# A linear-attention and two-layer expert kernel: decayed state on ScalarE from the ninth block on, a new step list, and another order at the end

## The chip, the cores and the metric

The kernel runs on one core of one Trainium2 chip. The metric is the device time of one execution in microseconds (us). Of the kernel before there are three timed runs, 505.46, 508.73 and 507.02 us, median 507.02. One further execution, of 505.58 us, was profiled; every row below is from it.

## The reference

Three things follow on each other. First, for 4 sequences and 8 heads of 768 tokens and 48 channels, a recurrent attention with a decay per channel:

```
cur   = (u * k_t) outer v_t
y_t   = r_t @ (state + cur)
state = w_t[:, None] * state + k_t outer v_t
```

Its output, 3072 tokens of 384 channels, goes through `h = x @ w_in` (384 to 2048), `g = h * cos(h)` and `x = g @ w_out`. Last comes a soft mixture of 8 experts with 4 slots each: `logits = x @ phi`; a softmax over all tokens gives each slot a mean of the tokens, each expert does `max(slot @ w1, 0) @ w2` (384 to 1024 to 384), and a softmax over the slots, token by token, mixes the 32 slot outputs into the output, 3072 x 384.

All inputs are float32 but `w_in`, `w_out` (float64, read as pairs of int32 and converted on the chip).

## The kernel before, in words

**Tiles and stages.** The 3072 tokens are 24 blocks of 128; a sequence has six blocks, a block two chunks (c) of 64 tokens. Two blocks make one of 12 groups of the softmax. Work on a block has three parts.

- *Attention of block j*: loads of r, k, v, w (`lr`, `lk`, `lv`, `lz`, `lw`, on SP's queue), transposes (`wT`, `rT`, `kT`, `kN` on PE), two scans of the decay on DVE (`scan`, `sp`), scaled keys and queries (`ks`, `L`), the chunk's inner products (`A`, then `mask`), the chunk's contribution to the state (`U` on PE). The state is carried by three small steps: `z` (line 250 on, the multiplication in L257) multiplies the state by the chunk's decay, `st` (L265, DVE) adds `U` to it, `rz` (L262, two ACT copies) puts z beside v for the product `y` (L276, PE). At the start of a sequence z is a memset (L254).
- *First layer of block t*: four quarters q of 512 columns. `h` (L430 to 432, nine PE matmuls), `turns` (L445, ACT), `rest` (L449, DVE), `cos` (L453, ACT), `mul` (L457, DVE), transposes `gT` (L464, PE), their copy `gc` (L470, ACT; some of the last on DVE), and `l` (L479, PE), the logits through a product of `w_out` and `phi`. `h` has two PSUM banks until nearly the end.
- *Softmax of group g*: `sum`, `lc`, `max`, `exp`, `dT`, `dc`, `ltok`; `E` (L575, PE) adds the tokens up with their weights, and `es` (L581, DVE) keeps the running sum `e_sb` and (L583) its divisor `st_s`. For the last group E and its update come in two halves (`E.11.0`, `E.11.1`, `esl.11.0`, `esl.11.1`).

**The order.** No planner runs: HEAD is a list of some 1900 steps written out in the file. Each step issues its instructions at its place, and each of the five engines (PE, DVE, ACT, POOL, and SP, which issues the DMAs) works through its own in that order. So an instruction waits for its data and for every earlier one on its engine. The name of a step holds its block, and then the chunk, quarter or part. The first steps also decode the weights: `raw` (load), `q` and `abs` (ACT), `d2a` (L343) and `d2b` (L348) on DVE, `whi`, `wn`, `wc` for `w_in`; `oT`, `oc`, `om` and others for `w_out`.

**The end.** After HEAD comes a second ordered part. PE adds up the divisor (`sum`, L729), transposes `e_sb` (L732), multiplies by `w_out` (L742) and transposes the slots' inputs (L749). `hidden(e)` (L761) does the first layer of expert e in 24 matmuls; `hidden_t(i)` takes the relu of four experts (L768, ACT), transposes it (L770, PE) and copies it (L772). `weights` (L719 to 721) rounds the token weights of one of four sets and one of two halves into `cr`, with a copy on ACT, DVE and POOL each. `expert_out(i, e)` (L801) is the second layer of expert e in 16 matmuls, for the columns 0 to 255 (i = 0) or 256 to 383 (i = 1). `slots_out` and `slots_round` (L808, L813, L814) sum it up and split it into a rounded part and a rest. `outputs(i, n0)` (L832, L834) mixes the slots for two tiles of 128 tokens (i = 0) or four (i = 1), copies the bank to `ob` (L841) and issues a store (L842). The expert weights are loaded whole, 1536 KB each (`load_e`, L642 and L646): numbers 0 to 5 when attention's memory is free (`att`), 6 to 10 into the memory of `w_in` and of x (`we`), 11 to 13 after HEAD, 14 and 15 during `hidden`.

## Time and profile before

| | |
|---|---|
| runs, us | 505.46, 508.73, 507.02; median 507.02 |
| profiled execution, us | 505.58 |
| its span, first to last instruction, us | 503.9 |
| busy: PE, DVE, ACT, POOL, us | 470.7, 420.2, 329.6, 101.9 |
| mean granted TensorE clock | 0.993 |
| largest groups: `h`, three lines, us | 118.2, 112.4, 112.7 |
| moved by DMA, MB | 67.47 |

Busy time is the time in which an engine ran at least one instruction. A matmul's end is modelled, so a busy PE is not one at its peak. Idle time counts only on the engine that is the bound in its stretch; so the tables by stretch say more than the shares over the whole span. A line's "idle before" is the time for which its engine stood still ahead of it, and the name behind the arrow is what ended that.

### The profile page before, as it was taken

The numbers are of one execution on the slowest core, as the hardware profiler recorded it, in microseconds if no ns is written. First come the engines' busy times: TensorE is split into PE (matmuls) and PEld (weight loads), VectorE is DVE, ScalarE is ACT, GpSimd is POOL, SyncE is SP. The second block draws the span as 40 slices with busy tenths as digits, with TensorE's granted clock in tenths as the row PEclk, the third lists the DMA queues.
The fourth block names the chain that finished last, engine by engine and source line by source line (L and its number), as shares of the span: only waits on it lengthen the run. The fifth ranks groups of instructions, "written<-read, shape, count | busy, mean of one in ns | idle before, by whom it ended". The sixth has DMA issues, their size and how long they took to land.

```text
span 503.9 us, 15604 instructions
## 1 busy us (share of the span) xinstructions
PE 470.7 (93%) x6521; PEld 369.3 (73%) x6521; DVE 420.2 (83%) x820; ACT 329.6 (65%) x724; POOL 101.9 (20%) x127
## 2 busy tenths in 40 slices
...
GB/s 220 307 259 240 142 206 163 101 50 81 35 92 27 103 2 124 67 43 62 57 89 56 23 75 48 50 95 64 49 22 27 407 277 57 110 404 305 398 138 276
DMA packets 145157, 67.47 MB, mean 134 GB/s; under 512 B 127168, under 2 KB 133568, under 8 KB 145088
## 3 DMA queue, kind: packets, MB, share of 16 engines
...
q14 instruction: 18, 0.15, 0.1%
...
## 4 chain that ended last, share of the span: by engine, by line
PE 66%; DVE 21%; ACT 6%; DMA 3%; issue 2%; SPq 0%; DVEq 0%; ACTq 0%
PE h L430 10%; PE h L432 9%; PE h L431 9%; PE gT L464 7%; PE l L479 4%; PE y L276 4%; PE E L575 3%; DVE lt L223 3%; DVE g L449 3%; DVE g L457 2%; PE A L197 2%; PE hps L761 2%; PE so L801 2%; DVE pt L159 2%; PE U L248 2%
## 5 line engine op out<-in xcount | busy, mean ns | idle before, releaser
L430 PE MATMUL h<-wu,x 128*128 128x512 f32 (+1 forms) x288 | 118.2, 411 | 1.0 <-DVE g L457 0.7
L432 PE MATMUL h<-wu,x 128*128 128x512 f32 (+1 forms) x288 | 112.7, 391 | 0.0
L431 PE MATMUL h<-wu,x 128*128 128x512 f32 (+1 forms) x288 | 112.4, 390 | 0.0
L453 ACT ACTIVATE g<-g,half_pi 128x512 f32<-128x512 f32 x97 | 69.4, 719 | 37.0 <-DVE g L449 36.3
L445 ACT ACTIVATE g<-h 128x512 int32<-128x512 f32 x96 | 56.9, 595 | 45.1 <-PE h L432 40.6
L457 DVE TENSOR_TENSOR g<-g,h 128x512 f32<-128x512 f32 x96 | 64.9, 679 | 13.2 <-ACT g L453 12.1
L449 DVE SCALAR_TENSOR_TENSOR g<-g,h 128x512 f32<-128x512 int32 (+1 forms) x96 | 64.6, 677 | 9.6 <-ACT g L445 8.6
L430 PEld LDWEIGHTS h<-wu,x 128*128 128x128 f32 x288 | 54.2, 188 | 15.0 <-DVE g L457 4.0
L211 POOL TENSOR_SCALAR_AFFINE_SELECT lt<-bo 64x512 f32<-64x512 f32 x48 | 36.6, 763 | 140.9 <-ACT bo L239 71.5
L432 PEld LDWEIGHTS h<-wu,x 128*128 128x128 f32 x288 | 54.1, 188 | 11.9
L431 PEld LDWEIGHTS h<-wu,x 128*128 128x128 f32 x288 | 54.3, 188 | 9.3
L470 ACT COPY gt<-gT 128x512 f32<-128x512 f32 x89 | 52.1, 585 | 13.1 <-PE gT L464 9.9
L464 PE MATMUL gT<-cs,g 128*128 128x128 f32 x384 | 58.9, 278 | 0.4 <-issue 0.4
L164 POOL TENSOR_TENSOR ru<-rn,u_b 128x384 f32<-128x384 f32 x24 | 25.8, 1074 | 145.4 <-DMA rn<-in_r_dram 72.6
L464 PEld LDWEIGHTS gT<-cs,g 128*128 128x128 f32 x384 | 43.8, 141 | 8.9 <-issue 3.0
L262 ACT COPY rzs<-z 64x192 f32<-64x192 f32 x96 | 33.5, 349 | 1.8 <-DVE z L257 1.0
L180 DVE TENSOR_TENSOR lt<-rT,pt 64x512 f32<-64x512 f32 x48 | 32.8, 684 | 1.8 <-PE rT L136 0.6
L223 DVE COPY_PREDICATED lt<-cs,A 64x256 f32<-64x256 uint32 x72 | 32.2, 447 | 2.2 <-PE A L197 0.7
L479 PE MATMUL l<-gt,p_sb 128*32 128x128 f32 x768 | 31.9, 276 | 0.3 <-DVE gt L470 0.3
L151 DVE TENSOR_TENSOR_SCAN qt<-wf,one_b 128x520 f32<-128x520 f32 x24 | 31.1, 1296 | 0.6 <-ACT wf L146 0.5
L159 DVE TENSOR_TENSOR_SCAN pt<-wf,ini_f 128x520 f32<-128x520 f32 x24 | 31.1, 1295 | 0.1
L165 POOL TENSOR_TENSOR ru<-ru,kn 128x384 f32<-128x384 f32 x24 | 29.8, 1240 | 3.1 <-PE y L276 1.3
(168 smaller groups left out, 770.4 us busy)
## 6 DMA issues: line engine op xcount, KB each, us to landing
we<-in_moe_w_dram SPq DMA_DIRECT2D x16, 1536.0 KB, 10.2
...
```

The lines of the kernel that those rows point to most:

```text
L159: nc.vector.tensor_tensor_scan(pt, wf[:, 0:NS * SEG], ini_f, 0.0, ALU.mult, ALU.add)
L223: nc.vector.copy_predicated(out=lt[j % 2][h, a, c::2], mask=mask[h].bitcast(U32).unsqueeze(1).to_broadcast([64, HP, C]), data=ps[a][o, 0:HP])
L430: nc.tensor.matmul(half[:, f], lhsT=xh[:, c, :], rhs=wh, start=(c == 0), stop=False)
L431: nc.tensor.matmul(half[:, f], lhsT=xl[:, c, :], rhs=wh, start=False, stop=False)
L432: nc.tensor.matmul(half[:, f], lhsT=xh[:, c, :], rhs=wl, start=False, stop=(c == KD - 1))
L445: nc.scalar.activation(gt.bitcast(I32), hp, AF.Copy, bias=0.25, scale=1.0 / TWO_PI)
L449: nc.vector.scalar_tensor_tensor(out=gt, in0=gt.bitcast(I32), scalar=-TWO_PI, in1=hp, op0=ALU.mult, op1=ALU.add)
L453: nc.scalar.activation(gt, gt, AF.Sin, bias=half_pi[:, 0:1])
L457: nc.vector.tensor_tensor(out=gt, in0=gt, in1=hp, op=ALU.mult)
L464: nc.tensor.transpose(ps[:, m * 128:(m + 1) * 128], gt[:, m * 128:(m + 1) * 128], ident)
L470: (nc.vector.tensor_copy if n >= ATT and n % 8 in (1, 2, 5) else nc.scalar.copy)(gt_t[t, q], pend.pop(("gT", t, q)))
L479: nc.tensor.matmul(lps_t[g][32 * m:32 * m + 32, o:o + TB], lhsT=p_sb[:, 4 * q + m, :], rhs=gt[:, m * 128:(m + 1) * 128], start=first, stop ...
```

## The change

z, the decayed state, is made by four ACT activations (one for each pair of heads, with the decay as their scale) in place of one DVE multiplication, from block 8 (the ninth) on. The step list is another order of the same steps, with one new step, `late0`, which frees the memory of `gt` and of x and loads expert weights number 11 within HEAD; 12 and 13 follow after HEAD as before. The set LOW has the same members in another order, and the condition in `s_e` means the same as before.

At the end, `hidden_t(0)` stands ahead of the first four `weights`, the other four `weights` stand behind `hidden_t(1)`, and that has two `expert_out` ahead of it. The first four tiles of the columns 0 to 255 are stored one by one. DVE and ACT take turns at the copies in another order. `slots_rest` is split off and moved behind one more portion. The experts of the columns 256 to 383 are spread in pairs between the portions 5, 6 and 7. Tiles 0 to 19 are stored in column parts as before; the last four tiles are made in whole rows of 384 columns, two tiles at a time with the even and the odd tokens apart, so that a partition holds two neighbouring tokens and stores 3 KB in one run.

```diff
@@ -41,6 +41,7 @@
     NTT = NT // 128
     NTW = 6
     NLATE = 3
+    JZ = 8
     JA = 6
     NSPLIT = 4
     ATT = 77
@@ -54,7 +55,8 @@
     b_stack = ctx.enter_context(ExitStack())
     sm_p = b_stack.enter_context(tc.tile_pool(name="sm", bufs=2, side="right"))
     g_p = b_stack.enter_context(tc.tile_pool(name="g", bufs=NGB, side="right"))
-    gt_p = b_stack.enter_context(tc.tile_pool(name="gt", bufs=16 - NGB, side="right"))
+    t_stack = b_stack.enter_context(ExitStack())
+    gt_p = t_stack.enter_context(tc.tile_pool(name="gt", bufs=16 - NGB, side="right"))
     ps_stack = ctx.enter_context(ExitStack())
     ps_h = ps_stack.enter_context(tc.tile_pool(name="ps_h", bufs=2, space=PSUM))
     ps_t = ps_stack.enter_context(tc.tile_pool(name="ps_t", bufs=1, space=PSUM))
@@ -254,7 +256,11 @@
             nc.vector.memset(z, 0.0)
         else:
             pc = segs(q_t[j][0], 1, 1).rearrange("p (s c) j -> p s c j", c=2)
-            nc.vector.tensor_tensor(out=z, in0=st_state, in1=pc[:, :, c, :].to_broadcast([128, HP, D]), op=ALU.mult)
+            if j < JZ:
+                nc.vector.tensor_tensor(out=z, in0=st_state, in1=pc[:, :, c, :].to_broadcast([128, HP, D]), op=ALU.mult)
+            else:
+                for p in range(HP):
+                    nc.scalar.activation(z[:, p], st_state[:, p], AF.Copy, scale=pc[:, p, c])
         z_t[j, c] = z
 
@@ -630,7 +636,7 @@
         nc.gpsimd.memset(one_b[:, NS * SEG:NS * SEG + 1], 1.0)
         def close_decode():
             d_stack.close()
-            x2_p.append(b_stack.enter_context(tc.tile_pool(name="x2", bufs=1, side="right", reuse_waits="tile")))
+            x2_p.append(t_stack.enter_context(tc.tile_pool(name="x2", bufs=1, side="right", reuse_waits="tile")))
 
         wt = {}
         late = {}
@@ -659,10 +665,14 @@
         def wide(idx):
             load_e(idx, *((x_p, "x01") if idx == NTW + 4 else (wu_p, f"wu{idx - NTW}")))
 
+        def early_late():
+            t_stack.close()
+            load_e(NTW + 5, ctx.enter_context(tc.tile_pool(name="late0", bufs=1, reuse_waits="tile")), "late")
+
         def exp_table():
             nc.scalar.activation(half_pi[:, 1:2], half_pi[:, 0:1], AF.Exp)
 

...
@@ -680,12 +690,12 @@
         zs = fin0.tile([128, KD, NE * 36], F32, name="zs")
         et = fin0.tile([128, 4, 128], F32, name="et")
         late_a = ctx.enter_context(tc.tile_pool(name="late_a", bufs=1, side="right", reuse_waits="tile"))
-        late_b = ctx.enter_context(tc.tile_pool(name="late_b", bufs=NLATE - 1, side="right", reuse_waits="tile"))
+        late_b = ctx.enter_context(tc.tile_pool(name="late_b", bufs=NLATE - 2, side="right", reuse_waits="tile"))
         fin = ctx.enter_context(tc.tile_pool(name="fin", bufs=1, side="right", reuse_waits="tile"))
         tw_p = late["tw"]
         nc.gpsimd.memset(zs, 0.0)
-        for i in range(NLATE):
-            load_e(NTW + 5 + i, late_a if i == 0 else late_b, "late")
+        for i in range(1, NLATE):
+            load_e(NTW + 5 + i, late_a if i == 1 else late_b, "late")
         ps_stack.close()
         pr_ = ctx.enter_context(tc.tile_pool(name="pr", bufs=8, space=PSUM, reuse_waits="tile"))
 
@@ -780,15 +790,12 @@
                 hidden(e)
             sr = tw_p.tile([128, 3072], F32R, tag="tw", name="sr")[0:96, 0:DM]
             cr = tw_p.tile([128, NT], F32R, tag="tw", name="cr")[0:96].rearrange("p (j b t) -> p j b t", j=4, b=NB)
+            hidden_t(0)
             for j in range(2):
                 for b in range(2):
                     weights(cr, j, b)
-            hidden_t(0)
             for e in range(5, NE):
                 hidden(e)
-            for j in range(2, 4):
-                for b in range(2):
-                    weights(cr, j, b)
 
             ops = [pb(f"so{i}") for i in range(2)]
 
@@ -808,23 +815,32 @@
                 nc.tensor.matmul(pend["sp", i], lhsT=stack[:, 0:96], rhs=so[:, cols], start=True, stop=True)
 
             def slots_round(i):
+                cols = parts[i]
+                nc.scalar.copy(sr[:, cols], pend["sp", i])
+
+            def slots_rest(i):
                 cols, sp = parts[i], pend.pop(("sp", i))
                 h = slice(2 * SL, 3 * SL)
-                nc.scalar.copy(sr[:, cols], sp)
                 nc.vector.tensor_tensor(out=sr[h, cols], in0=sp[h], in1=sr[h, cols].bitcast(F32), op=ALU.subtract)
 
+            NA = 20
             obs = {}
 
-            def outputs(i, n0, tile_=None):
+            def buf(i, j):
+                q = (j // 6) if i == 0 else 2
+                if (i, q) not in obs:
+                    n = parts[i].stop - parts[i].start
+                    obs[i, q] = wu_p.tile([128, 6, 512 // n, n], F32, tag=f"wu{q}", name=f"ob{i}_{q}")
+                return obs[i, q][:, j % 6]
+
+            def outputs(i, n0, single=None):
 
                 cols = parts[i]
                 n = cols.stop - cols.start
                 nt = 512 // n
-                t0, t1 = (0, nt) if tile_ is None else (tile_, tile_ + 1)
+                t0, t1 = (0, min(nt, NA - n0 * nt)) if single is None else (single, single + 1)
                 ps = pb(f"o{i}_{n0}_{t0}").rearrange("p (t f) -> p t f", t=nt)[:, 0:t1 - t0]
-                if n0 % 6 == 0 and t0 == 0:
-                    obs[i] = wu_p.tile([128, 6, nt, n], F32, tag=f"wu{n0 // 6 if i == 0 else 2}", name=f"ob{i}_{n0}")
-                ob = obs[i][:, n0 % 6, t0:t1]
+                ob = buf(i, n0)[:, t0:t1]
                 for t in range(t0, t1):
                     tt = n0 * nt + t
                     if tt < 4:
@@ -832,18 +848,29 @@
                         nc.tensor.matmul(ps[:, t - t0], lhsT=cf[:, tt * 128:(tt + 1) * 128], rhs=so[:, cols], start=True, stop=True)
                     else:
                         nc.tensor.matmul(ps[:, t - t0], lhsT=cr[:, tt // NB, tt % NB, :], rhs=sr[:, cols], start=True, stop=True)
-                if tile_ is not None and n0:
-                    nc.vector.tensor_copy(ob, ps)
-                    if t1 < nt:
-                        return
-                    ob, t0 = obs[i][:, n0 % 6], 0
-                else:
-                    (nc.vector.tensor_copy if n0 % 2 else nc.scalar.copy)(ob, ps)
+                (nc.scalar.copy if (n0 if single is None else single) % 2 else nc.vector.tensor_copy)(ob, ps)
                 nc.sync.dma_start(out[(n0 * nt + t0) * 128:(n0 * nt + t1) * 128, cols].rearrange("(t p) f -> p t f", p=128), ob)
 
+            crf = cr.rearrange("p j b t -> p (j b t)")
+
+            def rows(k):
+
+                if "r" not in obs:
+                    obs["r"] = wu_p.tile([128, NTT // 2 - NA // 2, 2, DM], F32, tag="wu3", name="obr")
+                ob = obs["r"][:, k - NA // 2]
+                for i in range(2):
+                    ps = pb(f"r{k}_{i}")[:, 0:DM]
+                    nc.tensor.matmul(ps, lhsT=crf[:, 256 * k + i:256 * k + 256:2], rhs=sr, start=True, stop=True)
+                    (nc.scalar.copy if i else nc.vector.tensor_copy)(ob[:, i], ps)
+                nc.sync.dma_start(out[256 * k:256 * k + 256, :].rearrange("(p i) f -> p (i f)", i=2), ob.rearrange("p i f -> p (i f)"))
+
             expert_out(0, 0)
+            expert_out(0, 1)
             hidden_t(1)
-            for e in range(1, NE):
+            for j in range(2, 4):
+                for b in range(2):
+                    weights(cr, j, b)
+            for e in range(2, NE):
                 expert_out(0, e)
             nc.scalar.copy(so[:, parts[0]], ops[0][:, 0:256])
             expert_out(1, 0)
@@ -852,115 +879,118 @@
             slots_round(0)
             outputs(0, 0, 1)
             outputs(0, 1, 0)
+            slots_rest(0)
             outputs(0, 1, 1)
             for n0 in range(2, 5):
                 outputs(0, n0)
-            for e in range(1, 4):
-                expert_out(1, e)
-            for n0 in range(5, 9):
+            for n0, es in ((5, (1, 2)), (6, (3, 4)), (7, (5, 6))):
+                for e in es:
+                    expert_out(1, e)
                 outputs(0, n0)
-            for e in range(4, NE):
-                expert_out(1, e)
+            expert_out(1, 7)
             nc.vector.tensor_copy(so[:, parts[1]], ops[1][:, 0:128])
-            for n0 in range(9, 12):
-                outputs(0, n0)
+            outputs(0, 8)
+            outputs(0, 9)
             slots_out(1)
             slots_round(1)
-            for n0 in range(6):
+            slots_rest(1)
+            for n0 in range(NA // 4):
                 outputs(1, n0)
+            for k in range(NA // 2, NTT // 2):
+                rows(k)
 HEAD = """
-raw.i.1 q.i.1 cs raw.i.0 lw.0 abs.i.1 q.i.0 z.0.0 d2a.i.1 lk.0 neg wT.0 d2b.i.1 lw.1 abs.i.0 d2a.i.0 kT.0 whi.1 wf.0 misc wn.1.0 wT.1 d2b.i.0 scan.0
-lr.0 whi.0 rz.0.0 ks.0 sr.0 kN.0 sp.0 raw.i.3 wc.1.0 ksn.0 rT.0 wf.1 raw.i.2 ru.0 q.i.3 wn.1.1 lv.0 lk.1 abs.i.3 L.0 wn.0.1 wn.0.0 wc.0.1 lr.1 raw.i.4
-scan.1 A.0 d2a.i.3 wc.1.1 wc.0.0 q.i.2 d2b.i.3 bo.0 lz.0 d2a.i.2 U.0 bs.0 st.0.0 kT.1 z.0.1 lw.2 lv.1 raw.o.0 D.0 raw.i.6 sr.1 abs.i.2 st.0.1 lk.2
...
-turns.21.1 gc.20.3 mul.21.0 mul.21.2 h.22.3 h.22.1 turns.22.3 rest.21.1 gT.21.0 att cos.21.1 rest.22.3 gT.21.2 E.9.1 cos.22.3 gc.21.0 l.20.3
-turns.22.1 mul.21.1 l.21.0 mul.22.3 gc.21.2 gT.21.1 gc.21.1 h.22.0 l.21.1 es.9 l.21.2 turns.22.0 l.21.3 rest.22.0 h.23.3 sum.10 lc.10 rest.22.1
-cos.22.1 we.9 mul.22.1 cos.22.0 gT.22.3 h.23.2 turns.23.3.0 max.10 exp.10 mul.22.0 cmb.1.5 gT.22.0 xt.10 turns.23.3.1 gc.22.3 xr.10 xd.10 turns.23.2
-gT.22.1 dT.10 gc.22.0 rest.23.3.1 rest.23.2 ltok.10 dc.10 h.23.0 rest.23.3.0 cos.23.3.0 cos.23.2 E.10.0 mul.23.3.0 cos.23.3.1 mul.23.2 h.22.2
-turns.23.0 rest.23.0 h.23.1 we.10 cos.23.0 turns.22.2 gc.22.1 mul.23.0 rest.22.2 mul.23.3.1 gT.23.0 l.22.0 cos.22.2 l.22.1 turns.23.1 mul.22.2
-rest.23.1 gc.23.0 gT.22.2 l.23.0 gc.22.2 gT.23.2 we.6 cos.23.1 gc.23.2 l.22.2 l.22.3 mul.23.1 gT.23.1 gT.23.3 gc.23.3 we.8 tab gc.23.1 l.23.1 l.23.2
-l.23.3 sum.11 we.7 lc.11 E.10.1 max.11 quart.11 cmb.2.5 exp.11 dT.11 dc.11 es.10 E.11.1 esl.11.1 E.11.0 ltok.11 esl.11.0 cmb.1.6 cmb.2.6
+raw.i.1 raw.i.0 z.0.0 abs.i.1 q.i.1 cs d2a.i.1 q.i.0 neg abs.i.0 lw.0 raw.i.3 d2b.i.1 d2a.i.0 d2b.i.0 lk.0 whi.1 lr.0 wT.0 wn.1.0 wf.0 q.i.3 scan.0
+wn.1.1 lw.1 misc wc.1.0 whi.0 lv.0 wc.1.1 sr.0 raw.i.2 lk.1 kT.0 ru.0 sp.0 lr.1 rz.0.0 rT.0 d2a.i.3 ks.0 abs.i.3 wn.0.0 wT.1 wc.0.0 kN.0 d2b.i.3 L.0
+wf.1 wn.0.1 ksn.0 bo.0 bs.0 scan.1 U.0 st.0.0 q.i.2 D.0 raw.i.4 A.0 abs.i.2 z.0.1 lz.0 lw.2 sr.1 wc.0.1 st.0.1 d2a.i.2 ru.1 kT.1 raw.o.0 d2b.i.2 ks.1
...
+turns.21.2 mul.21.1 h.22.3 gT.21.0 gc.21.3 cmb.0.6 rest.21.2 gT.21.1 l.20.2 cos.21.2 l.20.3 E.9.1 gc.21.0 turns.22.0 l.21.0 mul.21.2 cmb.2.5
+turns.22.3 gc.21.1 rest.22.0 gT.21.2 rest.22.3 cos.22.3 mul.22.3 gc.21.2 h.22.1 turns.22.1 cos.22.0 att rest.22.1 l.21.1 l.21.2 l.21.3 es.9 cos.22.1
+h.23.2 sum.10 lc.10 mul.22.1 mul.22.0 turns.23.2 max.10 h.23.3 rest.23.2 exp.10 h.23.0 xt.10 turns.23.3.1 we.10 xr.10 xd.10 turns.23.3.0 cos.23.2
+dT.10 gT.22.0 gT.22.3 rest.23.3.0 mul.23.2 dc.10 gc.22.0 cos.23.3.0 ltok.10 E.10.0 rest.23.3.1 cos.23.3.1 mul.23.3.1 turns.23.0 gT.22.1 rest.23.0
+h.22.2 gc.22.1 cos.23.0 mul.23.3.0 h.23.1 mul.23.0 gT.23.0 l.22.0 l.22.1 turns.22.2 rest.22.2 gc.22.3 cos.22.2 mul.22.2 gT.22.2 turns.23.1 rest.23.1
+gc.23.0 we.6 gT.23.2 l.23.0 gc.22.2 cos.23.1 l.22.2 gc.23.2 l.22.3 we.9 mul.23.1 gT.23.1 gT.23.3 gc.23.1 l.23.1 we.8 we.7 gc.23.3 l.23.2 l.23.3 late0 sum.11
+lc.11 max.11 E.10.1 es.10 tab quart.11 exp.11 dT.11 cmb.2.6 dc.11 E.11.0 esl.11.0 E.11.1 esl.11.1 ltok.11 cmb.1.6
 """
```

## Rows read from the trace of the kernel before

**Rows 1.** The page's part 1: busy time, share of the span, instructions.

```profile
PE 470.7 (93%) x6521; PEld 369.3 (73%) x6521; DVE 420.2 (83%) x820; ACT 329.6 (65%) x724; POOL 101.9 (20%) x127
```

**Rows 2.** Busy time by stretch: from:to, length, engines (instructions), granted clock, DMA share, GB/s.

```profile
0.00:50.00 50.00, 32.96 (x404) 23.57 (x405) 41.01 (x55) 37.70 (x67) 14.45 (x31) 1.00 1.07 257
50.00:450.00 400.00, 395.26 (x5450) 316.47 (x5448) 358.22 (x712) 273.65 (x612) 80.82 (x86) 1.00 0.43 98
450.00:460.00 10.00, 6.71 (x87) 3.62 (x81) 5.64 (x20) 4.18 (x14) 0.82 (x1) 1.00 0.79 291
460.00:496.30 36.30, 35.76 (x589) 25.60 (x588) 14.69 (x35) 13.97 (x34) 5.85 (x9) 1.00 0.81 298
496.30:504.00 7.70, 0.00 (x0) 0.00 (x0) 0.64 (x1) 0.09 (x1) 0.00 (x0) 0.53 0.82 230
```

**Rows 3.** PE's waits from 50 to 450 us: in total, times, longest.

```profile
PE h L430 <- DVE g L457: 0.7, 2, 0.6
...
PE dT L549 <- DVE dl L541: 0.2, 1, 0.2
```

**Rows 4.** Groups by line: shapes, count, busy us, mean ns, idle before.

```profile
L257 DVE TENSOR_TENSOR z<-st_state,qt 128x192 f32<-128x192 f32 x44 | 16.8, 382 | 1.1 <-DVE ini_f L155 0.4
...
L239 ACT COPY bo<-bo 64x4 f32<-64x4 f32 x48 | 9.3, 193 | 3.1 <-DVE bo L234 2.0
...
L526 ACT ACTIVATE z<-dl,nb 128x65 f32<-128x65 f32 (+1 forms) x11 | 3.9, 351 | 0.4
...
L522 ACT ACTIVATE al<-dl,nb 128x1 f32<-128x1 f32 x1 | 0.3, 278 | 0.0
```

**Rows 5.** Busy time by stretch, blocks 8 to 23 of the attention.

```profile
165.00:395.00 230.00, 226.87 (x3211) 182.08 (x3210) 211.44 (x439) 151.05 (x341) 48.40 (x54) 1.00 0.37 66
```

**Rows 6.** PE's waits from 0 to 60 us.

```profile
PE kT L136 <- DVE st_state L265: 2.1, 2, 2.0
...
PE rT L136 <- DVE ks L186: 1.4, 1, 1.4
```

**Rows 7.** The timeline at the last group: start us, us, engine, line, operation, [idle before].

```profile
456.31 1.93 PE L575 MATMUL E<-g,dt 128*32 128x256 f32 x32 [0.51 <-ACT dt L556]
...
458.50 0.48 DVE L581 SCALAR_TENSOR_TENSOR e_sb<-e_sb,al,E 128x256 f32<-128x256 f32 x1
...
458.89 0.21 DVE L583 SCALAR_TENSOR_TENSOR st_s<-st_s,al,sg 128x1 f32<-128x1 f32 x1
...
459.25 0.35 PE L729 MATMUL sum<-st_s,cs 128*128 128x1 f32 x2 [1.01 <-DVE st_s L583]
```

**Rows 8.** The timeline at the two relus: weight loads of the transposes.

```profile
471.50 0.32 PEld L770 LDWEIGHTS hT<-cs,wo_sb 128*128 128x128 f32 x2 [0.48 <-ACT wo_sb L768]
...
476.82 0.32 PEld L770 LDWEIGHTS hT<-cs,wo_sb 128*128 128x128 f32 x2 [0.41 <-ACT wo_sb L768]
```

**Rows 9.** The outputs: stretches, then timeline, then the chain (start us, us, what).

```profile
484.00:491.00 7.00, 7.00 (x120) 6.18 (x124) 3.25 (x6) 3.26 (x7) 0.00 (x0) 1.00 0.51 165
491.00:496.00 5.00, 4.89 (x60) 4.50 (x52) 3.20 (x6) 2.11 (x5) 0.00 (x0) 1.00 1.04 345
497.00:502.00 5.00, 0.00 (x0) 0.00 (x0) 0.00 (x0) 0.00 (x0) 0.00 (x0) 0.50 1.05 289
...
485.14 14.83 SPq L842 DMA_DIRECT2D out_dram<-ob  x19
...
496.25 0.69 DVE L841 COPY ob<-o 128x512 f32<-128x512 f32 x1 [0.20 <-PE o L834]
...
487.15 1.45 PE so L801 x48
```

**Rows 10.** A stretch of the expert weights' loads.

```profile
470.00:480.00 10.00, 10.00 (x172) 5.75 (x168) 4.07 (x10) 3.92 (x10) 3.44 (x8) 1.00 1.01 389
```

**Rows 11.** Waits over the span: in total, times, longest.

```profile
ACT g L445 <- PE h L432: 40.6, 41, 2.3
...
ACT g L453 <- DVE g L449: 36.3, 48, 2.1
```

More of the change, by code (lines that the diff above doesn't have):

```diff
@@ new lines @@
+lw.10 cos.4.0 A.8 h.4.2 lk.10 D.8 sum.1 gT.4.1 mask.8 mul.4.0 turns.4.2 kT.9 lc.1 lv.8 gc.4.1 lv.9 rest.4.2 max.1 cos.4.2 mul.4.2 ru.10 exp.1 kN.8
+gT.4.0 h.4.3 scan.9 turns.4.3 xt.1 st.7.1 xr.1 h.5.0 gc.4.0 xd.1 ksn.8 dT.1 gT.4.2 ks.9 rz.7.1 bo.10 rest.4.3 turns.5.0 ltok.1 dc.1 U.8 sr.9 l.4.0
+z.8.0 cos.4.3 rest.5.0 st.8.0 mul.4.3 y.7 E.1.0 cos.5.0 z.8.1 mul.5.0 gc.4.2 sp.9 rz.8.1 lz.9 ru.9 xh.7 lw.11 wT.10 wf.10 h.5.1 st.8.1 h.6.1 rz.8.0
+gT.4.3 scan.10 kN.9 xl.7 rT.9 turns.5.1 E.1.1 turns.6.1 ksn.9 l.4.1 rest.5.1 rest.6.1 sr.10 cos.5.1 l.4.2 lv.10 y.8 gc.4.3 bo.9 L.9 mul.5.1 U.9 h.5.2
@@ new lines @@
+mul.8.0 bo.13 gc.7.0 h.8.1 rest.7.2 wf.13 cos.7.2 gT.7.3 lz.11 kN.12 D.12 ksn.12 L.12 lv.13 cmb.0.2 mul.7.2 l.7.0 E.2.1 xh.10 cmb.0.3 lk.14 turns.8.1
+U.12 rest.8.1 st.12.0 gc.7.3 h.8.2 cos.8.1 xl.10 gT.7.2 lw.14 z.12.1 lr.14 A.12 l.7.1 gc.7.2 lz.12 scan.13 l.7.2 turns.8.2 mul.8.1 bs.13 rest.8.2
+st.12.1 rz.12.1 l.7.3 mask.12 cos.8.2 sr.13 gT.8.1 h.8.3 sum.3 es.2 mul.8.2 gc.8.1 turns.8.3 wT.14 kT.13 rest.8.3 lc.3 cos.8.3 lw.15 gT.8.0 h.9.1
+ks.13 mul.8.3 z.13.0 max.3 h.9.0 kN.13 lk.15 gc.8.0 sp.13 exp.3 rT.13 xt.3 gT.8.2 xr.3 turns.9.1 lr.15 wf.14 ru.14 xd.3 ksn.13 dT.3 rest.9.1 ltok.3
```

156 lines of the change are left out of this document (74 added, 82 removed).

## The prediction

> **What bounds the kernel now.** I read the engines' shares first: TensorE (PE) is busy 470.7 of 503.9 us, VectorE (DVE) 83%, ScalarE (ACT) 65% [rows 1]. An average hides where the other 33 us are, so next comes the table by stretch [rows 2]. Of PE's 33.2 us of idle time 17.0 lie in the first 50 us (data arrive and weights are decoded), 4.7 in the 400 us from 50 to 450, 3.3 in the softmax's end (450 to 460), 0.5 in the experts and outputs (460 to 496.3), and 7.7 after PE's last matmul, when only copies and DMAs are left. So the long middle is bound by PE's own work; nothing that relieves another engine can give back more than 4.7 us there. The waits of PE in that stretch come next: ten kinds, the largest 0.7 us, and the five that DVE ended (the first and the last are shown) add up to 2.6 [rows 3]. The head is bound by DMA and decode, the end by a chain of single steps and then by the queue of output DMAs.
>
> The profiled execution took 505.58 us, 1.68 more than its span. The runs' median is 507.02, so 1.44 above the execution that I sum against; I add these 1.44 at the end.
>
> **Part 1, the decayed state on ACT.** For blocks 8 to 23 z is made twice a block; blocks 12 and 18 start a sequence and keep a memset, so 30 of the 44 tensor_tensors go. Each took 0.382 us on DVE [rows 4]: 11.5 us off DVE. Each is replaced by four ACT activations of 128x48 whose scale is read per partition. The trace has none of this shape. From below: a 64x4 copy, 0.193 us, hardly more than the cost of an instruction. From above: a 128x65 activation with a bias per partition, 0.351. Between lies 128x1 with such a bias, 0.278 [rows 4]; the slope (0.073 us over 64 columns) gives 0.278 + 47 x 0.00114 = 0.33 for 48 columns. I take 0.33, since it has both the operand and the length. A z then costs 1.33 us of ACT (0.77 to 1.40), 30 cost 40 us (23 to 42).
>
> These blocks run from about 165 to 395. There ACT is busy 151.1 of 230 us and DVE 211.4 [rows 5]. After the change ACT has 191 (83%), DVE 200 (87%). Both stay below PE's 226.9, so on sums alone PE remains the bound and hides both; if that cover goes, the price is that of the second rival below. What stands behind a z on ACT is turns, cos, gc and rz of nearby blocks, and PE waits for these through the two h banks. The wait that z brings to ACT (for DVE's st) was DVE's own order before; the rz that follows it now comes from the same engine. What can be gained is PE's idle time: at most 4.7 us, and 2.6 us of it was ended by DVE. I take -0.8 for a DVE that is 5 points emptier; bounds -4.7 and, from the rival, +6.8.
>
> **Part 2, the new order.** All steps but one are the same, in another order. In the head DVE still has the same set of steps ahead of mask 0, L 1, z 1.0 and the decode of w_in part 4 (I added up the work ahead of each in both lists). The keys of block 0 are loaded behind 768 KB of weights; ks 0, which needs them, has moved behind sr, sp and a decode step on DVE, about 3 us, which covers it. Later, ks 2, for which PE waited 1.4 us [rows 6], has 1.05 us less DVE work ahead of it, and rest 0.0 has 1.3 us more. The kinds of PE's waits here, after the first, are of 1.1 to 2.1 us (the longest and that for ks are shown) [rows 6]. I take 0, with one wait gone or one more as bounds: -1.5 to +1.5. On SP's queue we.10 stands ahead of we.6 and we.9 and so need not queue behind a later bank's release; late0 starts a 1.5 MB load ahead of the last group's softmax and not after it. PE waited for no expert weights, so this gives 0; it also costs nothing, since the only issues behind late0 on SP are the other late weights and the outputs.
>
> **Part 3, the softmax's end.** Now E 11.0 and its update come first, ltok after both updates. Before, the second e_sb update stood behind two ltok copies until 458.50, then st_s, and PE's sum started at 459.25 [rows 7]. PE's E ended at 458.24; in the new order the second update starts then, at about 458.28, ends at 458.76, and st_s is done by then: sum at 458.9, -0.35.
>
> **Part 4, experts.** Twice the transposes hT waited for a relu on ACT, 0.48 and 0.41 us of weight-load idle time [rows 8]; matmuls already in the pipe hid about half. The first relu now stands ahead of the weight copies on ACT (hps 0 is complete one expert earlier), the second has another 16 matmuls ahead of its transposes. Both go: -0.4. The weight copies moved back have the matmuls of six experts to hide behind.
>
> **Part 5, outputs.** From 491 the DMA engines are full: 345 GB/s while packets are 1 KB (columns 0 to 255), 289 with 512 B (the rest); SP's 19 issues run to 499.97, 3 us after the last copy [rows 9]. So the end is set by bytes and by the gaps before 491, not by PE. Before: 3.15 MB / 345 + 1.57 MB / 289 = 9.1 + 5.4 = 14.5 us. After, 20 tiles in columns and 4 whole, in runs of 3 KB: 2.62 / 345 + 1.31 / 289 = 12.1, and 0.79 MB at a rate that no write here shows. Bounds: 345 as for 1 KB (2.3 us) and the 389 of the expert loads, whose runs are 3 or 4 KB (2.0 us) [rows 10]; I take 2.0, the nearest in size. Together 14.1: -0.4. The gaps (a share of 0.51 in the 7 us up to 491, 3.4 us of idle DMA) change both ways: two 128 KB portions instead of one of 256 KB leave about 0.5 us sooner, but the subtraction in sr moved behind a DVE copy (0.4 us later), and pairs 5, 6 and 7 each stand behind two experts, 32 matmuls or 0.97 us at 1.45 per 48 [rows 9], plus its own, while the queue eats a pair (262 KB at 345) in 0.76. I take 0; bounds -1 and +1.
>
> **Sum.** -0.8 + 0 - 0.35 - 0.4 - 0.4 = -1.95: 503.6 for an execution like the profiled one, **505.0** as a median.
>
> **Rivals.** (a) **The middle closes up**: with DVE at 87% all 4.7 us of PE's idle time go, and the end gives its 1.15: 507.02 - 5.9 = 501.2; with a wait less in the head 499.7. For it: a DVE at 92% of these 230 us has few places to catch up. Against it: only part of PE's waits end at DVE.
>
> (b) **ACT's order takes over, slower.** ACT waits on average 40.6/41 = 0.99 us ahead of a turns for PE and 36.3/48 = 0.76 ahead of a cos for DVE [rows 11]. A z of 1.33 put into such a gap overshoots it by 0.34 to 0.57 us, and with it the turns or cos that frees an h bank. If all 30 overshoots reached PE it would lose 13.6 us, if half, 6.8. It decides from the point where PE finds no h bank ready. Half: 507.02 - 1.15 + 6.8 = 512.7. For it: ACT's in-order queue now holds seven or eight extra instructions a block. Against it: before, ACT's idle time was 79 of 230 us, and z stands well ahead of the y that needs it.
> The Trainium skill, "ScalarE: Activation LUTs", section "Rules for kernel authors", says that a multiply belongs on VectorE and not on ScalarE, which speaks against this change; its figures in "What ACT_TABLE_LOAD costs" (186 ns, 93 more for a pointer operand, 0.833 per column) give 0.32 us a piece as an estimate, and the sum by that would differ by about 0.1 us of ACT a block. The rows agree with the price (0.382 on DVE against 1.33), but whether a dearer place matters depends on which engine binds, and there the rows show PE.
>
> (c) **The change does not do what it says**: the DMA stream is as long, because the later pairs open as many gaps as the early portions close, and the middle was PE's all along: 507.0.
>
> **Chances.** A measurement of this kernel tells about 1% from no change. Forecast 0.53, (c) 0.15, (a) 0.18, (b) 0.14. Faster by over 1% (under 501.9) takes (a) and the lower end of the forecast: 0.22. Slower by over 1% (over 512.1): most of (b), 0.12. Within: 0.66. The range reaches from (a), 500.0, to the larger part of (b), 511.0; the forecast's own is 502.5 to 508, from the bounds of parts 2 and 5 and the spread of the runs (505.46 to 508.73).
>
> **What would show it.** z pieces of 0.33 us on ACT and no tensor_tensor z after block 7; ACT at 83%, DVE at 87% in the same stretch; PE's idle time from 50 to 450 near 4 us (under 1: rival a; 10 or more, ended by ACT: rival b). PE's sum 0.3 us sooner after the second E; no wait at hT; a last stretch of DMA near 389 GB/s; a stream of about 14 us with 3 us of gaps. I am wrong if PE's idle time in the first 50 us moves by more than 2 us, or if the z activations come out far from 0.33.

## The result and the profile after

The kernel after takes **509.15 us** (median of 7 runs, 508.52 to 510.29) against 507.02 (505.46 to 508.73): ratio 1.0052, 95% interval 1.0034 to 1.0071. Forecast were 505.0. It is slower by 2.1 us in the medians (0.42%; the ratio puts it at 0.52%), within the 1% that had the largest chance, but on the other side of no change. The profiled execution took 509.42 us, 3.84 more than that of before; so this pair of traces shows more than the medians do.

The engines' shares on the page of the kernel after, then stretches of it (from:to, length, engines with instructions, granted clock, DMA share, GB/s):

```profile
PE 476.1 (94%) x6517; PEld 371.1 (73%) x6517; DVE 411.3 (81%) x791; ACT 357.0 (70%) x844; POOL 96.8 (19%) x127
```

```profile
0.00:50.00 50.00, 35.59 (x402) 25.10 (x402) 41.40 (x56) 38.16 (x70) 14.51 (x31) 0.93 1.06 258
50.00:450.00 400.00, 393.63 (x5399) 315.22 (x5399) 346.46 (x680) 298.18 (x726) 75.62 (x86) 1.00 0.42 94
...
165.00:395.00 230.00, 225.94 (x3110) 179.94 (x3103) 201.45 (x404) 171.68 (x441) 46.96 (x54) 1.00 0.34 60
...
488.10:507.70 19.60, 11.67 (x164) 9.38 (x162) 7.11 (x13) 5.62 (x12) 0.00 (x0) 0.85 0.76 242
505.00:506.00 1.00, 0.00 (x0) 0.00 (x0) 0.00 (x0) 0.00 (x0) 0.00 (x0) 0.50 1.00 390
```

Against [rows 2, 5]: DVE went down as forecast (201.5, 87.6% of the 230 us), ACT went up by 20.6 and not by 40, and PE stood still for 6.4 us from 50 to 450 where it had been 4.7 and "near 4" was forecast. In the profiles the last `h` begins 3.4 us later than before (449.99 against 446.57), the softmax's end takes 0.4 of that back, and the outputs add 0.8. Where PE waited from 50 to 450, against [rows 3] (total, times, longest):

```profile
PE h L436 <- DVE g L463: 2.2, 4, 1.0
PE y L282 <- issue: 1.2, 1, 1.2
PE U L250 <- DVE lt L225: 0.7, 1, 0.7
PE E L581 <- ACT dt L562: 0.5, 2, 0.3
...
```

These are single places. Two of them on the timeline (start us, us, engine, line, operation, [idle before]): `h` of block 13 waits for a bank that `mul` 13.0 has to free, and `mul` stands on DVE behind a scan that took 2.07 us beside work of POOL, where it takes 1.23 with POOL idle (last section); and `U` 18 waits for `mask` 17.

```profile
287.47 1.01 POOL L166 TENSOR_TENSOR ru<-rn,u_b 128x384 f32<-128x384 f32 x1 [0.58 <-DMA rn<-in_r_dram]
287.51 2.07 DVE L153 TENSOR_TENSOR_SCAN qt<-wf,one_b 128x520 f32<-128x520 f32 x1
...
289.51 0.66 DVE L463 TENSOR_TENSOR g<-g,h 128x512 f32<-128x512 f32 x1
...
290.22 0.50 PE L436 MATMUL h<-wu,x 128*128 128x512 f32 x1 [0.99 <-DVE g L463]
...
308.44 1.84 DVE L225 COPY_PREDICATED lt<-cs,A 64x256 f32<-64x256 uint32 x4
...
310.43 0.67 PE L250 MATMUL U<-vn,ksn 64*64 64x48 f32 x30 [0.69 <-DVE lt L225]
```

### The profile page after: what moved, and what is told of

Read it like the earlier page. It is cut to its first block, busy times and chain, and to the rows that moved or that the text cites. A ratio compares the mean times of both kernels' runs of the same rounds, so it can differ in the third digit from the quotient of the medians.

```text
span 507.7 us, 15677 instructions
## 1 busy us (share of the span) xinstructions
PE 476.1 (94%) x6517; PEld 371.1 (73%) x6517; DVE 411.3 (81%) x791; ACT 357.0 (70%) x844; POOL 96.8 (19%) x127
## 4 chain that ended last, share of the span: by engine, by line
PE 61%; DVE 22%; ACT 10%; issue 3%; DMA 2%; SPq 0%; POOL 0%; DVEq 0%; ACTq 0%; POOLq 0%
PE h L436 9%; PE h L438 8%; PE h L437 8%; PE gT L470 6%; PE l L485 4%; DVE g L463 3%; PE y L282 3%; DVE lt L225 2%; DVE g L455 2%; PE E L581 2%; PE A L199 2%; DVE lt L182 2%; PE so L808 2%; PE hps L771 2%; DVE qt L153 2%
## 5 line engine op out<-in xcount | busy, mean ns | idle before, releaser
L436 PE MATMUL h<-wu,x 128*128 128x512 f32 x288 | 119.0, 413 | 2.4 <-DVE g L463 2.2
L438 PE MATMUL h<-wu,x 128*128 128x512 f32 x288 | 112.8, 392 | 0.0
L437 PE MATMUL h<-wu,x 128*128 128x512 f32 x288 | 112.3, 390 | 0.0
L459 ACT ACTIVATE g<-g,half_pi 128x512 f32<-128x512 f32 (+1 forms) x97 | 69.5, 719 | 27.9 <-DVE g L455 26.8
L463 DVE TENSOR_TENSOR g<-g,h 128x512 f32<-128x512 f32 (+1 forms) x96 | 64.8, 679 | 19.7 <-ACT g L459 19.0
L451 ACT ACTIVATE g<-h 128x512 int32<-128x512 f32 (+1 forms) x96 | 56.8, 594 | 30.9 <-PE h L438 28.4
L166 POOL TENSOR_TENSOR ru<-rn,u_b 128x384 f32<-128x384 f32 x24 | 24.2, 1008 | 91.7 <-DMA rn<-in_r_dram 46.7
L263 ACT ACTIVATE z<-st_state,qt 128x48 f32<-128x48 f32 x120 | 30.1, 323 | 2.7 <-DVE st_state L271 2.5
L153 DVE TENSOR_TENSOR_SCAN qt<-wf,one_b 128x520 f32<-128x520 f32 x24 | 30.5, 1269 | 1.5 <-ACT wf L148 1.3
L161 DVE TENSOR_TENSOR_SCAN pt<-wf,ini_f 128x520 f32<-128x520 f32 x24 | 29.6, 1235 | 0.2
```

The source lines that it names most:

```text
L436: nc.tensor.matmul(half[:, f], lhsT=xh[:, c, :], rhs=wh, start=(c == 0), stop=False)
L437: nc.tensor.matmul(half[:, f], lhsT=xl[:, c, :], rhs=wh, start=False, stop=False)
L438: nc.tensor.matmul(half[:, f], lhsT=xh[:, c, :], rhs=wl, start=False, stop=(c == KD - 1))
L451: nc.scalar.activation(gt.bitcast(I32), hp, AF.Copy, bias=0.25, scale=1.0 / TWO_PI)
L459: nc.scalar.activation(gt, gt, AF.Sin, bias=half_pi[:, 0:1])
L463: nc.vector.tensor_tensor(out=gt, in0=gt, in1=hp, op=ALU.mult)
```

## Experiments

Ratios are to the kernel before, run on the same chip in the same job, with the 95% interval. The "old list" is the step list of before, the "old end" its second ordered part.

### Cutting the change into its parts

**new_list_old_end**: the new list, `late0` and z on ACT; relus, weight copies and outputs as before.

```diff
-            hidden_t(0)  ...  rows(k)        # the new second ordered part
+            weights(cr, j, b) ...  hidden_t(0)  ...  outputs(1, n0)   # the old one
```

> The kernel after with the second ordered part (relus, weight copies, outputs) as it was before; list, early load and z on ACT stay. Theory L (the new list costs the time: +3.4 us at the last h, taken back by 0.4 in the softmax's end): span about 3 us over that of before, ratio 1.004 to 1.007, and the stretch from the second E's update to the end as long as before. Theory O (the output order costs it): within 0.6 us of before, 1.000 to 1.001. Theory Z (z on ACT costs it): like L here, so this run only parts O from the other two.

508.44 us, **1.0044** (1.0029 to 1.0060). The list with z on ACT carries most of the loss; the end alone can't.

**old_list_new_end**: the same cut the other way round, old list with z on DVE.

> The kernel before with only the new second ordered part (relu ahead of the weight copies, split slots_rest, experts in pairs, last four tiles in whole rows). Theory L: +0.8 us (0.1 off at the relus, 0.9 more at the outputs, the gap of the DMA queue near 497), ratio 1.001 to 1.003. Theory O: +2 us or more, 1.004 and over. My prediction's parts 4 and 5: -0.8 us, 0.998 to 0.999. Theory Z: 1.000 to 1.002, says nothing.

507.60 us, **1.0024** (1.0011 to 1.0037). The end costs 1.2 us where I forecast -0.8. The two ratios add up to 1.0068, within the errors of 1.0052; on the new list the end costs 0.08% (1.0052 - 1.0044), on the old 0.24%.

**new_list_z_dve**: the kernel after with `JZ = 99`.

```diff
-    JZ = 8
+    JZ = 99
```

> The kernel after with all z on DVE as before (JZ = 99), everything else new. Theory Z: the loss in the middle goes, so about +0.5 us on before, ratio 1.000 to 1.002, under the kernel after by 2 us or more. Theory L: the loss stays and DVE has 11 us more work in the blocks 8 to 23, so as slow as after or slower, 1.005 to 1.012, with PE's idle time from 50 to 450 us at 6 us or over.

514.22 us, **1.0151** (1.0122 to 1.0181), above the range of theory L even. **old_list_z_act**: the kernel before with z on ACT alone.

```diff
+            if j < JZ:   # JZ = 8
                 nc.vector.tensor_tensor(out=z, in0=st_state, in1=..., op=ALU.mult)
+            else:
+                for p in range(HP):
+                    nc.scalar.activation(z[:, p], st_state[:, p], AF.Copy, scale=pc[:, p, c])
```

> The kernel before with z on ACT from block 8 on, and nothing else: old list, old end. Theory Z (and rival b of the prediction): PE waits for turns and st, +2 to +6.8 us, ratio 1.004 to 1.013. Theory L: within 1 us of before, 0.998 to 1.002, PE's idle time from 50 to 450 us between 4 and 6 us, z pieces 0.32 us. Part 1 of the prediction: -0.8 us, 0.998.

516.27 us, **1.0197** (1.0170 to 1.0224): 10 us, more than theory Z gave. So both theories fall as I had put them: z on ACT costs 2% in the old list, and taking it off ACT costs 1% in the new one. List and place of z act together and can't be priced one by one. In old_list_z_act, from 165 to 395: the stretch, then the waits of DVE and ACT, then one place on the timeline:

```profile
165.00:395.00 230.00, 219.68 (x3090) 174.90 (x3089) 195.40 (x394) 165.97 (x424) 45.65 (x52) 1.00 0.34 57
```

```profile
DVE g L462 <- ACT g L458: 12.9, 18, 2.2
DVE st_state L270 <- ACT z L262: 7.2, 6, 1.8
...
ACT z L262 <- DVE st_state L270: 5.2, 3, 2.6
```

```profile
369.09 0.35 DVE L270 TENSOR_TENSOR st_state<-U,z 128x192 f32<-128x192 f32 x1
...
369.48 1.01 ACT L262 ACTIVATE z<-st_state,qt 128x48 f32<-128x48 f32 x4 [1.21 <-DVE st_state L270]
370.40 0.56 ACT L475 COPY gt<-gT 128x512 f32<-128x512 f32 x1
370.86 0.72 ACT L458 ACTIVATE g<-g,half_pi 128x512 f32<-128x512 f32 x1
371.01 0.64 PE L484 MATMUL l<-gt,p_sb 128*32 128x128 f32 x16 [1.11 <-ACT gt L475]
...
371.61 0.69 DVE L462 TENSOR_TENSOR g<-g,h 128x512 f32<-128x512 f32 x1 [2.17 <-ACT g L458]
```

PE's idle time is 10.3 us here (before 3.1). ACT stands 1.21 us at z for `st`, is busy with z for 1.01, and `gc` and `cos` of another quarter come behind it: PE and DVE both wait for them. Elsewhere DVE stands at `st` for z, 7.2 us in all, and what is queued behind on DVE waits too.

### What of z on ACT costs the time

**old_list_z_mid**: 29 of the 30 z moved to the middle between the steps that they depend on and that depend on them (the thirtieth can't be moved so).

```diff
-st.j-1.1 z.j.0 ... st.j.0
+st.j-1.1 ... z.j.0 ... st.j.0
```

> old_list_z_act (1.0197) with 29 of the 30 z moved within the list to the middle between the st that they wait for and the st or rz that waits for them; nothing else. Theory H (ACT stands at z until DVE's st is done, with gc, cos and turns of other quarters queued behind, at 370 us 1.2 us of wait and 1.0 of z, then PE 1.1 for gc): at least 4 us back, ratio 1.012 or less. Theory W (the 30 us of work on ACT cost it wherever they stand): 1.017 or more.

515.56 us, **1.0167** (1.0148 to 1.0186): 1.5 us back of 10, which the errors of the two runs just cover, close to theory W's bound and far from H's. But the move changed little of what H speaks of: ACT's wait at z for `st` went from 5.2 to 3.5 us, DVE still stands at `st` for 5.8, and by the start times in the two traces z begins a median of 2.1 us behind the end of the `st` ahead of it, 2.0 before the move. So this run leaves H short of its forecast and does not refute it. **old_list_z_act_rz_pool** tried the work itself:

```diff
-            nc.scalar.copy(rzs[...], z_t[j, c][...])
+            (nc.scalar.copy if j < JZ else nc.gpsimd.tensor_copy)(rzs[...], z_t[j, c][...])
```

> old_list_z_act (1.0197) with rz of the blocks 8 to 23 as two POOL copies in place of two ACT copies (0.35 us each): z still waits on ACT for st at the same places, but ACT's work in these blocks is about what it was before (30 us of z for 22 us of rz). Theory W (ACT's added work costs the time): most of the 10 us back, ratio 1.006 or less. Theory H (the wait at z's place in ACT's order costs it): 1.013 or more.

515.06 us, **1.0170** (1.0146 to 1.0194). ACT's busy time in the 230 us was back at 150.2 (before 151.1), and the loss stayed; DVE stood at `st` for 8.3 us. So it isn't ACT's load, and W falls. What is left is that z, a link of the chain `st`, z, `st`, has to take its turn in a queue where other work stands ahead of it and behind it, which is H in a wider form, or that z is longer. **old_list_z_pool** takes it off both engines:

```diff
+                nc.gpsimd.tensor_tensor(out=z, in0=st_state, in1=pc[...].to_broadcast([128, HP, D]), op=ALU.mult)
```

> The kernel before with the 30 z on POOL as one tensor_tensor each, old list, old end: DVE is relieved as in the kernel after and ACT has nothing new. If a DVE with 11.5 us less gives back what part 1 of the prediction took (0.8 us, at most 4.7): 0.991 to 0.998. If DVE's relief is worth nothing: 0.999 to 1.001. Rival P (POOL is in order too, and a longer z there delays st, or it slows DVE's scans beside it): 1.003 or more.

503.69 us, **0.9949** (0.9933 to 0.9966), faster than both kernels. Its group by line, the stretch, and DVE's wait at `st`:

```profile
L261 POOL TENSOR_TENSOR z<-st_state,qt 128x192 f32<-128x192 f32 x30 | 17.7, 591 | 139.6 <-DVE st_state L269 109.4 <-ACT rzs L266 20.9 <-ACT wf L147 7.6
```

```profile
165.00:395.00 230.00, 227.75 (x3221) 183.07 (x3213) 205.16 (x416) 152.81 (x345) 61.43 (x79) 1.00 0.37 70
```

```profile
DVE st_state L269 <- POOL z L261: 1.4, 2, 0.7
```

POOL stands ready (139.6 us of idle time ahead of z): z begins a median of 0.14 us behind the end of `st`, against 2.0 on ACT, and `st` waits for it 1.4 us in all. PE's idle time falls to 2.3. With z off DVE and not on ACT the old list gains 2.6 us, three times what I gave DVE's relief. **pool_four_pieces** then separates length from queue, on pool_end_sum (below):

```diff
-                nc.gpsimd.tensor_tensor(out=z, in0=st_state, ...)
+                for p in range(HP):
+                    nc.gpsimd.tensor_tensor(out=z[:, p], in0=st_state[:, p], ...)
```

> pool_end_sum (0.9929) with each z of the blocks 8 to 23 on POOL in four pieces of 128x48, as ACT has them, estimated at 0.8 to 1.1 us a z against 0.52 in one piece. Theory V (a z of 1 us lengthens the chain st, z, st, and DVE stands at st): most of ACT's loss comes here too, 1.003 or more, DVE's waits at st for z over 5 us. Theory Q (z stands in ACT's queue behind other work, and other work behind it, and that costs the time): 0.992 to 0.996, DVE's waits at st under 3 us.

505.61 us, **0.9987** (0.9976 to 0.9998), between the two ranges. DVE's wait at `st` for z is 3.2 us (1.4 in pool_end_sum), near theory Q's 3 and under V's 5.

```profile
L262 POOL TENSOR_TENSOR z<-st_state,qt 128x48 f32<-128x48 f32 x120 | 30.5, 286 | 133.2 <-DVE st_state L270 110.8 <-ACT rzs L267 20.5 <-ACT z L531 1.8
```

A z of 30.5/30 = 1.02 us, as long as ACT's 1.00, costs 0.58% (0.9987 - 0.9929) over one of 0.5. From POOL to ACT it was 2.48% (1.0197 - 0.9949). So about a quarter of ACT's price is the length of z (a tenth to two fifths with the errors). The rest is what is left over: z begins 0.14 us behind `st` here too, and 2.0 on ACT, so I put it down to z's turn in ACT's queue; no run takes away that turn alone.

### Where the new list loses

**new_list_moves_old_end**: three steps moved in new_list_old_end, at the places shown above.

```diff
-rest.13.0 h.13.3 scan.18 ... rest.13.3   U.18 gT.14.1   turns.20.1 y.22 ... gT.20.0
+rest.13.0 h.13.3 ... rest.13.3 scan.18   gT.14.1 U.18   turns.20.1 ... gT.20.0 y.22
```

> new_list_old_end (1.0044 of before) with three steps moved: scan 18 behind rest 13.3, U 18 behind gT 14.1, y 22 behind gT 20.0. Theory L (the 2.2 us are single stalls of the new list, at 290 us h on mul 0.99, at 310 us U on mask 0.69 and more inside U, at 410 us y on issue 0.7 to 1.2): all three go, 2.4 to 3.2 us off, ratio 0.998 to 1.000. Rival S (the slack of the other engines sets it and a stall taken away comes back a few steps on): 1.003 or more, PE's idle time from 50 to 450 us still over 5 us.

507.90 us, **1.0030** (1.0019 to 1.0042): 0.7 us back, within the errors of the two runs, and not 2.4 to 3.2. The waits at 290 and 310 us are gone, PE's idle time from 50 to 450 us falls from 5.6 to 4.3, and PE does its work from 275 to 313 us 1.3 us sooner; the wait on `issue` at `y` is 0.4 and was 0.7, with nothing gained behind it. Both theories miss: L by its time, S by PE's idle time, which it put over 5. The single stalls are about a third of the list's loss.

**new_list_z_pool**: the kernel after with z on POOL.

> The kernel after (1.0052) with the 30 z as one POOL tensor_tensor each (0.52 us). The new list with z on DVE gave 1.0151, with z on ACT 1.0052. If the new list itself costs the time, with z off both engines: 1.003 to 1.006, as after. If what is left of z's work on ACT costs it: 0.998 to 1.001 (DVE's relief, 0.5%, less the end, +0.24%). If the list is fitted to z on ACT in both ways: above 1.006.

509.24 us, **1.0050** (1.0030 to 1.0070). The new list is as fast with z on ACT as with z on POOL, as if it had been fitted to z's turn in ACT's queue: z begins as late behind `st` as in old_list_z_act (median 1.9 us), but DVE stands at `st` for 3.8 us, not 7.2. It is slow with both. Without the end (0.24%) it stands at 1.0026 where the old list with the same z has 0.9949: the list costs 0.77%, 3.9 us (about 1.5 either way, by the errors of the three ratios).

Adding up PE's matmuls, each kind at its mean spacing, and reading when the two reach the same sum: new_list_z_pool lies level with or up to 1.2 us ahead of old_list_z_pool to 290 us, then 1.0 behind at 313, 3.8 at 364, 5.0 at 413, and no more after. Two mixed lists test that place, both on pool_end_sum. **new_then_old** and **old_then_new** are cut ahead of `rest` 13.0 (286 us):

```diff
+new_then_old: the new list up to rest.13.0, then what is left in the old order
+old_then_new: the old list up to rest.13.0, then what is left in the new order
```

Neither has `late0`.

> pool_end_sum (0.9929) with the new list up to turns 13.0 (about 286 us) and all steps left in the order of the old list (its softmax's end as in the kernel after); no late0. Theory T (the new list loses its time after 286 us, 4 to 6 us by PE's work done at equal times): 0.991 to 0.995. Rival D (the loss is spread over the list, or comes with the state in which the first part leaves the engines): 0.998 or more.

> The other way round: the old list up to rest 13.0, then all steps left in the new order, z on POOL, the end as in pool_end_sum. Theory T: the late part of the new list brings its loss along, 1.001 to 1.006. Rival D: 0.997 or less.

505.08 us, **0.9976** (0.9963 to 0.9989), and 510.04, **1.0078** (1.0061 to 1.0096). Neither is in its range, because the seam costs by itself: at 290 and 296 us two stalls of 0.98 in the first, and in the second

```profile
286.32 1.48 PE L280 MATMUL y<-lt,rzs 128*32 128x64 f32 x52 [2.69 <-issue]
```

Behind the seam (from about 294 us on) PE in old_then_new falls 3 to 4 us further behind pool_end_sum, in new_then_old not at all; but the latter's outputs take 19.3 us where pool_end_sum's take 18.1. Their copies keep the same pace; what differs is a hole in the stream, since the sixth and the seventh store are issued 2.47 us apart and in pool_end_sum 0.55. The same place in both, new_then_old first:

```profile
488.00:490.00 2.00, 2.00 (x61) 1.87 (x62) 1.29 (x2) 1.01 (x2) 0.00 (x0) 1.00 0.18 57
```

```profile
487.20:489.20 2.00, 2.00 (x62) 1.86 (x64) 1.29 (x2) 1.00 (x2) 0.00 (x0) 1.00 0.83 272
```

Why the seventh is late isn't shown. So the late part of the new list does bring a loss along, as theory T had it, and without `late0`; its size is not clean.

### The end, and the parts that pay

**new_end_old_spread**: old_list_new_end with two things put back.

```diff
             slots_round(0)
+            slots_rest(0)
...
-            for n0, es in ((5, (1, 2)), (6, (3, 4)), (7, (5, 6))):  ...
+            experts 1 to 3, portions 5 to 8, experts 4 to 7, portion 9
```

> old_list_new_end (1.0024) with the subtraction right behind the rounding copy and the experts 1 to 3 and 4 to 7 in two rows as before; single stores, DVE first in the copies, whole rows and relus as in the kernel after. Theory G (the DMA queue's gaps cost it): gaps back to about 3.4 us, stream 0.4 shorter, ratio 0.998 to 1.000. Rival R (the rows or the earlier relus cost it): 1.002 or more, with the DMA engines idle no longer than before.

505.92 us, **0.9990** (0.9976 to 1.0004), against 1.0024. From the first output's issue to the end, old_list_new_end and then new_end_old_spread:

```profile
486.42:506.00 19.58, 11.67 (x164) 9.38 (x162) 7.11 (x13) 5.63 (x12) 0.00 (x0) 0.84 0.77 242
```

```profile
484.78:503.00 18.22, 10.71 (x164) 9.40 (x162) 7.01 (x13) 5.54 (x12) 0.00 (x0) 0.84 0.82 260
```

DMA busy 19.58 x 0.77 = 15.1 us and idle 4.5, against 14.9 and 3.3. Theory G holds: the gaps cost it, the whole rows don't. Which of the two things put back closed them isn't parted.

**pool_end_sum** is old_list_z_pool with this end and the new order of the softmax's end (`E.11.0 esl.11.0 E.11.1 esl.11.1 ltok.11`); **pool_all_blocks** has z on POOL from block 1 on as well.

> The parts that paid, on the old list: z on POOL from block 8 on (0.9949), the end of new_end_old_spread (0.9990) and the new order of the softmax's end (0.4 us in two profiles). If they add: 0.9949 - 0.0010 - 0.0008 = 0.993 (0.9915 to 0.995). If a gain in the middle is taken back by late expert weights: 0.995 or more, with a PE wait for DMA in the experts.

> pool_end_sum with z on POOL from block 1 on, 44 in place of 30. DVE is busy 107.6 of 115 us from 50 to 165, more than later, so if its relief counts by how full it is: 1 to 2 us under pool_end_sum, 0.989 to 0.992. If POOL (32 of these 115 us, with the decode's and the blocks' own steps in order) makes st wait: 0.995 or more.

503.17 us, **0.9929** (0.9903 to 0.9955), and 502.96, **0.9925** (0.9904 to 0.9945). The parts add up; the 14 further z give nothing that can be told. Both beat both kernels.

## Why the prediction was wrong

| z on | old list, old end | new list, new end |
|---|---|---|
| DVE | 1 | 1.0151 |
| ACT | 1.0197 | 1.0052 (the kernel after) |
| POOL | 0.9949 | 1.0050 |

**Part 2 is the step that failed, and part 5's gaps with it.** I costed the head's order and gave the whole list 0 (bounds 1.5); the middle I took for PE's own. Along the table: DVE's relief -2.6 us (POOL, old list), the list +3.9, ACT in place of POOL in the new list 0.1, the end +1.2; in all 2.6, or 0.52%. Each of these is a difference of ratios, good to 0.7 to 1.5 us. The other path through the table is as valid: z on ACT +10, the list -8.6 with the end at 1.2 (-7.8 by new_list_old_end itself). What doesn't depend on the path is that I priced list and z apart. That the measured time lies inside the range of 500.0 to 511.0 is no merit of the sum: the range was that wide for rivals (a) and (b), and neither came true as it stands.

**Part 1.** z's price was right (0.33; measured 0.323), but four in a row overlap by about 0.1 us at each join, so a z took 1.00 us of ACT and not 1.33. From the kernel after, by line:

```profile
L260 DVE TENSOR_TENSOR z<-st_state,qt 128x192 f32<-128x192 f32 x14 | 6.1, 434 | 0.1
L263 ACT ACTIVATE z<-st_state,qt 128x48 f32<-128x48 f32 x120 | 30.1, 323 | 2.7 <-DVE st_state L271 2.5
```

The Trainium skill, "ScalarE: Activation LUTs", section "What ACT_TABLE_LOAD costs", gave 0.32 us a piece as an estimate, and the trace agrees.

"The wait that z brings to ACT was DVE's own order before" was wrong: before, z and `st` stood in one queue, and DVE's waits show none at `st` for z; afterwards two queues wait for each other (7.2 and 5.2 us in old_list_z_act), and each holds up what stands behind. Rival (b) had that queue, but as an overshoot of z into gaps. Its sign holds in the old list, where it cost 10 us, between half of (b)'s overshoots (6.8) and all of them (13.6); in the new list that price is gone. The Trainium skill, "ScalarE: Activation LUTs", section "Rules for kernel authors", has a rule against a multiply on ScalarE: in the old list the rows agree (2.0% slower), in the new list z on DVE is the slower one.

**Part 3** was right. `sum` stood 1.01 us behind the second `E` [rows 7] and now follows it at 0.03; in its place the second `eT` waits for the `ltok` copies:

```profile
459.69 1.93 PE L581 MATMUL E<-g,dt 128*32 128x256 f32 x32 [0.51 <-ACT dt L562]
461.65 0.35 PE L739 MATMUL sum<-st_s,cs 128*128 128x1 f32 x2
...
462.75 0.44 PE L742 MATMUL eT<-cs,e_sb 128*128 128x128 f32 x2 [0.47 <-DVE ltok L568]
463.12 2.24 PE L752 MATMUL si<-wo_sb,et 128*32 128x256 f32 x32
...
467.80 6.68 PE L771 MATMUL hps<-we,zs 128*32 128x256 f32 x120
```

From E's end to the product `si` it is 1.50 us, and was 2.15; but `si` takes longer here, and to the experts' first matmul (`hps`, at 464.81 before) it is 6.18 us and was 6.57. Forecast -0.35, measured -0.39.

**Part 4** gave 0.1, not 0.4. I took half of the weight load's wait [rows 8] for a wait of PE. Its matmuls, whose ends are modelled, show none: before, those of the experts run to 471.49, and `hT` follows at 471.50.

```profile
464.81 6.68 PE L761 MATMUL hps<-we,zs 128*32 128x256 f32 x120
...
471.50 0.51 PE L770 MATMUL hT<-cs,wo_sb 128*128 128x128 f32 x2
```

Afterwards the relu no longer ends the load's wait, but the load comes no sooner:

```profile
473.26 0.38 ACT L778 ACTIVATE wo_sb<-hps 128x256 f32<-128x256 f32 x1 [4.15 <-PE hps L771]
...
474.41 0.32 PEld L780 LDWEIGHTS hT<-cs,wo_sb 128*128 128x128 f32 x2 [0.41 <-issue]
```

The 0.41 us stand there although the relu was done 0.77 us before the load; the profile names only `issue`, and what holds the load isn't shown.

**Part 5.** The stream was right: 18.76 us x 0.82 = 15.4 busy before, 19.60 x 0.76 = 14.9 after (-0.5; forecast -0.4), and the 3 KB rows ran at 390 GB/s (389 assumed [rows 10]). The gaps, whose change I set to 0 (bounds 1), went from 3.4 to 4.7 us. Before, the stream was

```profile
485.14:503.90 18.76, 10.96 (x168) 9.77 (x167) 7.19 (x13) 5.39 (x11) 0.00 (x0) 0.81 0.82 252
```

I had both causes, the subtraction and the pairs behind two experts, and set two early portions against them. In the kernel after:

```profile
489.40 0.42 DVE L824 TENSOR_TENSOR sr<-sp,sr 32x256 fp32r<-32x256 f32 x1
...
489.97 0.94 PE L850 MATMUL o<-sr,cr 96*128 96x256 f32 x6 [0.63 <-DVE sr L824]
...
495.28 0.58 ACT L851 COPY ob<-o 128x512 f32<-128x512 f32 x1 [2.30 <-PE o L850]
```

PE stood 0.63 us for the subtraction, and the copies came 1.4 us apart for a queue that eats a pair in 0.76. The early portions gave nothing back: the first store is issued 1.18 us behind the first `o` matmul, and was 1.14.

**The head.** PE's busy time in the first 50 us moved by 2.6 us, past the 2 that I had named as a sign of error. Half of it goes with the lower clock (below): with the same list and the clock at 1.00, new_list_z_pool has 34.23 us and moved by 1.3. In work done, added up as above, PE is not behind: at 50 us it stands 0.3 to 0.5 us ahead of before. So the sign was no sign of a loss.

**What stays open**: what the new list loses after 290 us beyond its single stalls, and what `issue` is at `y` (0.4 to 2.7 us in the traces of the new list, of old_list_z_mid and of the two mixed lists), where PE waits for nothing that the profile shows.
